# Second MLP's first layer: token tiles 0 and 1 as seven block products, accumulators kept in memory between stages

## The chip, the cores and the metric

One core of a Trainium2 chip. The metric is the time of one execution of the kernel on the device, in microseconds, lower is better. Before the change: median 592.0 us of 3 runs (591.9 to 592.14).

## The reference

`out = mlp2(mlp1(retention(q, k, v, lam)))` on 1536 tokens of width 512:

```
x = retention(q, k, v, lam)            # block-wise linear attention, 2 x 8 heads x 768 x 64
h = max(x @ w_in, 0);  x = (h * h) @ w_out          # first MLP:  512 -> 2048 -> 512
h = x @ w_in;          out = max(0.01 * h, h) @ w_out   # second MLP, leaky
```

The MLP weights come as 64-bit floats, everything else as 32-bit.

## The kernel before

**Precision.** A 32-bit operand is split into a high part (rounded to the matmul's format, `hi`) and the rest (`lo`); each product is three matmuls, hi x hi, hi x lo, lo x hi. ScalarE makes the high part, VectorE subtracts it from the source for the low part (`split`, L64).

**Tiling.** The tokens are three tiles of 512 (t = 0, 1, 2), the hidden width four stages of 512 columns (s = 0 to 3), for each of the two MLPs (l = 0, 1). `first(l, s, t)` (L379) makes a stage's hidden block: 4 column groups m x 4 inner blocks x 3 = 48 matmuls of 128x512 into four banks of the accumulator memory, each followed by the activation and the split into `ghi`, `glo`. `second` (L405) multiplies by the second weight, again 48 matmuls, and adds each of four banks to `acc`, which stays on chip over the stages.

**Order.** The list `line` (L446 to L451) sets the program: behind the first stage it alternates first of step i and second of step i-1, so that between a block's activation and its use a whole other tile of 48 matmuls lies. One step of weight work is put in at every fourth turn: `fetch` (L86) has SP load a quarter of a stage's weights (1024 KB of 64-bit words) and `converting` (L93) turns it into 32-bit hi and lo: on ScalarE the absolute value (L103) and the high part (L113), on VectorE seven operations on 128x1024, three of one input (L104, L105, L110) and four of two (L107, L111, L112, L114). The scheduler of the language orders each engine's instructions by its own estimate; TensorE and SP are in the written order only in the retention.

GpSimd works in the retention alone. Eight banks of accumulator memory are used in rotation (L58).

The functions that the diff touches follow with the line numbers of the profile.

## Time and profile before

| what | value |
|---|---|
| time, median of 3 runs | 592.0 us (591.9 to 592.14) |
| profiled execution: span from first to last instruction | 590.4 us |
| around the span (median less span) | 1.6 us |
| TensorE busy | 582.3 us, 99% |
| VectorE busy | 399.3 us, 68% |
| ScalarE busy | 253.3 us, 43% |
| GpSimd busy | 24.5 us, 4%, all before 60 us |
| granted TensorE clock, mean | 0.997 |

TensorE's busy time includes overlaps of pipelined matmuls; how fast it really goes is read from the distance between two matmuls in order of time. In the profile PE is TensorE, PEld its weight loads, DVE VectorE, ACT ScalarE, POOL GpSimd, SP the engine that issues the transfers.

### The profile page before, as it was taken

What the parts mean: (1) busy time and instruction counts of PE and PEld (TensorE: products, weight loads), DVE (VectorE), ACT (ScalarE), POOL (GpSimd) and SP (SyncE); (2) the same over time, 40 slices, a digit from 0 to 9 for tenths busy, and PEclk for the clock granted to TensorE, in tenths of its full rate; (3) what the DMA queues carried; (4) which work ended last, traced back from release to release, by engine and by line L of the source; (5) the groups of instructions that cost most, each with busy time, mean ns of one, the idle gap of its engine ahead of it and who ended that gap; (6) DMA issues with size and microseconds to landing.
All of it is one profiled execution on the core that took longest, in us unless ns stands there. A gap on an engine that the chain in (4) does not pass through costs nothing.

```text
span 590.4 us, 7683 instructions
## 1 busy us (share of the span) xinstructions
PE 582.3 (99%) x3147; PEld 485.9 (82%) x3147; DVE 399.3 (68%) x543; ACT 253.3 (43%) x379; POOL 24.5 (4%) x37
## 2 busy tenths in 40 slices
PE   7999999999999999999999999999999999999997
PEld 7888878888888888888888888888888888888886
DVE  3789499999979393856849793946779443344332
ACT  2344588458663372455373443536152223123120
POOL 2425000000000000000000000000000000000000
PEclk9999999999999999999999999999999999999999
DMA  8998133453343122040302212120400000000112
GB/s 175 240 211 205 67 101 113 153 180 115 124 142 89 54 72 71 2 143 0 143 1 72 71 68 75 46 98 1 142 1 0 1 0 2 0 1 0 72 53 90
DMA packets 57331, 47.17 MB, mean 80 GB/s; under 512 B 38216, under 2 KB 39504, under 8 KB 57296
## 3 DMA queue, kind: packets, MB, share of 16 engines
q1 hardware_dynamic: 56768, 46.41, 26.6%
q8 instruction: 25, 0.41, 0.3%
q10 hardware_dynamic: 528, 0.26, 0.2%
q14 instruction: 10, 0.08, 0.0%
HBM read 43.52 MB, written 3.15 MB: 79 GB/s over the span
## 4 chain that ended last, share of the span: by engine, by line
PE 94%; DVE 2%; DMA 1%; ACT 1%; issue 1%; POOL 0%; SPq 0%; POOLq 0%; ACTq 0%
PE ps L426 44%; PE ps L393 14%; PE ps L391 14%; PE ps L392 14%; PE ps L258 2%; PE ps L275 2%; PE ps L326 1%; DMA raw<-in_moe_w_in 1%; PE ps L324 1%; PE ps L299 1%; PE ps L184 1%; DVE glo L399 0%; ACT qT L262 0%; POOL kd L293 0%; SPq L62 0%
## 5 line engine op out<-in xcount | busy, mean ns | idle before, releaser
L391 PE MATMUL ps<-xhi,whi 128*128 128x512 f32 x384 | 149.6, 389 | 0.0
L393 PE MATMUL ps<-xhi,wlo 128*128 128x512 f32 x384 | 149.4, 389 | 0.2 <-DVE wlo L114 0.2
L392 PE MATMUL ps<-xlo,whi 128*128 128x512 f32 x384 | 149.4, 389 | 0.0
L431 DVE TENSOR_TENSOR acc<-ps,acc 128x512 f32<-128x512 f32 (+1 forms) x73 | 49.7, 681 | 61.9 <-PE ps L426 61.8
L393 PEld LDWEIGHTS ps<-xhi,wlo 128*128 128x128 f32 x384 | 72.1, 188 | 15.6 <-DVE wlo L114 0.6
L391 PEld LDWEIGHTS ps<-xhi,whi 128*128 128x128 f32 x384 | 72.1, 188 | 15.2 <-ACT whi L113 0.2
L392 PEld LDWEIGHTS ps<-xlo,whi 128*128 128x128 f32 x384 | 72.1, 188 | 15.0
L426 PE MATMUL ps<-wlo,ghi 128*128 128x512 f32 (+1 forms) x196 | 75.4, 385 | 0.0
L426 PE MATMUL ps<-whi,glo 128*128 128x512 f32 (+1 forms) x196 | 75.4, 385 | 0.0
L426 PE MATMUL ps<-whi,ghi 128*128 128x512 f32 (+1 forms) x196 | 75.4, 385 | 0.0
L401 ACT ACTIVATE r<-ps 128x512 f32<-128x512 f32 x48 | 28.7, 598 | 92.9 <-PE ps L393 92.8
L426 PE MATMUL ps<-ghi,whi 128*128 128x512 f32 x176 | 68.5, 389 | 0.0
L426 PE MATMUL ps<-glo,whi 128*128 128x512 f32 x176 | 68.5, 389 | 0.0
L426 PE MATMUL ps<-ghi,wlo 128*128 128x512 f32 x176 | 68.5, 389 | 0.0
L402 DVE TENSOR_TENSOR r<-ps,r 128x512 f32<-128x512 f32 x48 | 33.1, 689 | 33.0 <-ACT r L401 33.0
L396 ACT ACTIVATE r<-ps 128x512 f32<-128x512 f32 x48 | 28.5, 595 | 52.2 <-PE ps L393 51.7
L399 DVE TENSOR_TENSOR glo<-r,ghi 128x512 fp32r<-128x512 f32 x44 | 30.2, 688 | 30.4 <-ACT r L398 30.3
L114 DVE TENSOR_TENSOR wlo<-hb,whi 128x1024 fp32r<-128x1024 f32 x32 | 38.7, 1222 | 15.8 <-ACT whi L113 15.8
L113 ACT CAST whi<-hb 128x1024 fp32r<-128x1024 f32 x32 | 33.1, 1051 | 37.7 <-PE ps L426 27.4
L66 DVE TENSOR_TENSOR glo<-r,ghi 128x512 fp32r<-128x512 f32 x48 | 33.2, 691 | 22.2 <-ACT ghi L65 22.0
L65 ACT CAST ghi<-r 128x512 fp32r<-128x512 f32 x48 | 29.8, 621 | 37.5 <-DVE r L402 37.5
L103 ACT ACTIVATE hb<-raw 128x1024 f32<-128x1024 f32 x32 | 36.8, 1153 | 20.0 <-DMA raw<-in_moe_w_in 12.6
(78 smaller groups left out, 739.6 us busy)
## 6 DMA issues: line engine op xcount, KB each, us to landing
raw<-in_moe_w_in SPq DMA_DIRECT2D x16, 1024.0 KB, 5.5
raw<-in_moe_w_out SPq DMA_DIRECT2D x16, 1024.0 KB, 5.0
k<-in_k SPq DMA_DIRECT2D x12, 256.0 KB, 4.5
q<-in_q SPq DMA_DIRECT2D x12, 256.0 KB, 4.9
v<-in_v SPq DMA_DIRECT2D x12, 256.0 KB, 5.0
out<-acc SPq DMA_DIRECT2D x11, 256.0 KB, 2.0
DTr<-tab SPq DMA_DIRECT2D x1, 256.0 KB, 5.1
DTr<-tab ACTq DMA_DIRECT2D x1, 256.0 KB, 5.3
```

What stands on the lines that cost most here:

```text
L65: nc.scalar.copy(hi, src)
L66: nc.vector.tensor_tensor(out=lo, in0=src, in1=hi, op=ALU.subtract)
L103: nc.scalar.activation(hf, w_hi.bitcast(F32), AF.Abs)
L113: nc.scalar.copy(hi, hf)
L114: yield ve.tensor_tensor(out=lo, in0=hf, in1=hi, op=ALU.subtract)
L391: nc.tensor.matmul(ps, hi_w[:, kk, ms], xhi[t][:, kk], start=kk == 0, stop=False)
L392: nc.tensor.matmul(ps, hi_w[:, kk, ms], xlo[t][:, kk], start=False, stop=False)
L393: nc.tensor.matmul(ps, lo_w[:, kk, ms], xhi[t][:, kk], start=False, stop=kk == KD - 1)
L399: nc.vector.tensor_tensor(out=glo[:, m], in0=r, in1=ghi[:, m], op=ALU.subtract)
L402: nc.vector.tensor_tensor(out=r, in0=ps, in1=r, op=ALU.max)
L426: nc.tensor.matmul(ps, a, b, start=kk == 0 and n == 0, stop=kk == KF - 1 and n == 2)
L431: nc.vector.tensor_tensor(out=a, in0=ps, in1=a, op=ALU.add)
```

## The change

In the second MLP the first layer of tiles 0 and 1 is one job now, `first_pair(s)`. Weight and tokens are seen as 2 x 2 blocks: for each half h of a stage's columns (256) the weight blocks A11 to A22 (inner half j, 128 columns i), the tokens B11, B21 (tile 0, the two inner halves), B22 and B12 (tile 1). Four sums of weight blocks (S1 to S4) and four of token blocks (T1 to T4) are made, and seven products of six matmuls each take the place of eight. Their results are combined on VectorE in 32 bit: s1, s2 and r22 hold partial sums, and every block of tiles 0 and 1 is activated from there.

- `weight_sums` (in each stage, for each half) runs on GpSimd: four operations on 256 elements and two low parts on 512, with two high parts on ScalarE. `token_sums` (once, behind the first MLP) runs on GpSimd, four operations on 512 for each of two inner blocks, then splits on ScalarE and VectorE.
- The order of a stage is written out: in the first MLP `first` of tiles 0 and 1 by column halves, `second` of 0, `first` of 2, `second` of 1 and 2; in the second MLP `first_pair`, `second` of 0, `first` of 2, `second` of 1 and 2. At the end of the first MLP, `second` of tile 1 does column groups 0, 2, 1, then `first` of tile 2, then group 3, then `second` of tile 2. TensorE keeps the written order throughout.
- Weights are held by halves, w1 once, w2 three times; the conversion goes on one VectorE step at a time (`convert(1)` at each half group), except behind the last three pairs of products, and holds its last step until a buffer is free (`opened`).
- The second MLP's accumulators aren't kept on chip: after each stage each 128x512 block is written to memory (`spill`), and read back before the next stage's addition. A pool `fp` of nine 128x512 buffers serves all such plain values.

```diff
@@ converting
         yield ve.tensor_tensor(out=hf, in0=hf, in1=rf, op=ALU.add)
+        while key not in opened:
+            yield None
+        tags = (f"w1h{h}", f"w1l{h}") if n == 0 else ("w2h", "w2l")
+        bufs = 1 if n == 0 else 3
+        hi, lo = (wp.tile([P, 4 * CW], F32R, tag=tag, name=tag, bufs=bufs) for tag in tags)
         nc.scalar.copy(hi, hf)
...
         yield ve.tensor_tensor(out=lo, in0=hf, in1=hi, op=ALU.subtract)
+        if l == 1 and n == 0:
+            weight_sums(s, h, hf.rearrange("p (k f) -> p k f", k=k))
...
+    def weight_sums(s, h, w):
+        a = {(i, j): w[:, 2 * j:2 * j + 2, i * P:(i + 1) * P] for i in range(2) for j in range(2)}
+        both = late.tile([P, 2, 4, 2, P], F32R, tag=f"sw{h}", name=f"sw{h}")
...
+        po.tensor_tensor(out=f12[:, 0], in0=a[1, 0], in1=a[1, 1], op=ALU.add)
+        po.tensor_tensor(out=f12[:, 1], in0=f12[:, 0], in1=a[0, 0], op=ALU.subtract)
+        po.tensor_tensor(out=f34[:, 0], in0=a[0, 0], in1=a[1, 0], op=ALU.subtract)
+        po.tensor_tensor(out=f34[:, 1], in0=a[0, 1], in1=f12[:, 1], op=ALU.subtract)
+        for f, n in ((f12, 0), (f34, 2)):
+            nc.scalar.copy(both[:, 0, n:n + 2], f)
+            po.tensor_tensor(out=both[:, 1, n:n + 2], in0=f, in1=both[:, 0, n:n + 2], op=ALU.subtract)
+
+    def token_sums(j):
+        po = nc.gpsimd
+        a, b, c, d = x0f[j], x1f[j], x1f[j + 2], x0f[j + 2]
+        po.tensor_tensor(out=a, in0=b, in1=a, op=ALU.subtract)
+        po.tensor_tensor(out=b, in0=c, in1=b, op=ALU.subtract)
+        po.tensor_tensor(out=c, in0=c, in1=a, op=ALU.subtract)
+        po.tensor_tensor(out=d, in0=d, in1=c, op=ALU.subtract)
+        split(xhi[1][:, j], xlo[1][:, j], a)
+        for n, src in ((2, c), (3, b), (4, d)):
...
+            split(tt[n][:, 0, j], tt[n][:, 1, j], src)
+
+    def activate(l, src, r, ghi, glo):
...
+            if src is r:
+                nc.vector.scalar_tensor_tensor(out=r, in0=src, scalar=0.01, in1=src, op0=ALU.mult, op1=ALU.max)
+            else:
+                nc.scalar.mul(r, src, 0.01)
+                nc.vector.tensor_tensor(out=r, in0=src, in1=r, op=ALU.max)
+            nc.scalar.copy(ghi, r)
+        nc.vector.tensor_tensor(out=glo, in0=r, in1=ghi, op=ALU.subtract)
...
+    def first_pair(s):
...
+        def product(h, where, a, b, start=True):
+            if start:
+                ps[h, where] = bank()
+            (ah, al), (bh, bl) = w[h, a], x[b]
+            ops = []
+            for j in range(2):
+                ops += [(ah[:, j], bh[:, j]), (ah[:, j], bl[:, j]), (al[:, j], bh[:, j])]
+            three(ps[h, where], ops, start, True, not start)
+            return ps[h, where]
...
+        for h in both:
+            b = product(h, "A", "A11", "B11")
+            s1[h] = plain()
+            nc.scalar.copy(s1[h], b)
+            yield True
+        for h in both:
+            product(h, "B", "S2", "T2")
+            s2[h] = plain()
+            plus(h, s2[h], "B", s1[h])
+            yield True
+        for h in both:
+            product(h, "D", "A22", "T4")
+            yield True
+        for h in both:
+            product(h, "C", "S1", "T1")
+            yield True
+        for h in both:
+            product(h, "B", "S3", "T3", False)
+            plus(h, s1[h], "B", s1[h])
+            r22[h] = plain()
+            plus(h, r22[h], "C", s1[h])
+            plus(h, s1[h], "D", s1[h])
+            yield False
+        for h in both:
+            put(h, product(h, "A", "A12", "B21", False), plain(), 0, 0)
+            put(h, s1[h], s1[h], 1, 0)
+            yield False
+        for h in both:
+            product(h, "C", "S4", "B22", False)
+            plus(h, s2[h], "C", s2[h])
+            yield False
+        for h in both:
+            put(h, r22[h], r22[h], 1, 1)
+            put(h, s2[h], s2[h], 0, 1)
...
@@ second
+            if l == 1 and s and cs.start == 0:
+                spilled[m] = plain()
+                dma(spilled[m], spill[t][m])
...
+                if s == 0:
+                    spilled[m] = plain()
+                    nc.scalar.copy(spilled[m], ps)
+                else:
+                    a = spilled[m][:, cs]
+                    nc.vector.tensor_tensor(out=a, in0=ps, in1=a, op=ALU.add)
+                if last:
+                    r0 = t * TT + m * P
+                    dma(out[r0:r0 + P, cs], spilled[m][:, cs])
+                else:
+                    dma(spill[t][m], spilled[m])
...
+    def stage(l, s):
+        if (l, s) == (0, 0):
+            parts = [first(l, s, t, range(2)) for t in range(NTILE)]
+            parts += [first(l, s, t, range(2, 4)) for t in (0, 2, 1)]
+            return parts + [second(l, s, t) for t in (2, 0, 1)]
+        if l == 0:
+            parts = [first(l, s, t, ms) for ms in (range(2), range(2, 4)) for t in range(2)]
+        else:
+            parts = [first_pair(s)]
+        if (l, s) == (0, NS - 1):
+            return parts + [second(l, s, 0), second(l, s, 1, (0, 2, 1)), first(l, s, 2), second(l, s, 1, (3,)),
+                            second(l, s, 2)]
+        return parts + [second(l, s, 0), first(l, s, 2), second(l, s, 1), second(l, s, 2)]
```

**VectorE at the end of the products, second stage of the second MLP.** Before, the first layer of one tile: r is the activated block, glo its low part, hb, rb and wlo are weight conversion.

```order
L402 TENSOR_TENSOR r_3167<-ps_3154,r_3167 128x512
L66 TENSOR_TENSOR glo0_3104<-r_3167,ghi0_3103 128x512
L114 TENSOR_TENSOR wlo00_3322<-hb_3356,whi00_3321 128x4x256
L402 TENSOR_TENSOR r_3185<-ps_3172,r_3185 128x512
L114 TENSOR_TENSOR wlo00_3322<-hb_3435,whi00_3321 128x4x256
L66 TENSOR_TENSOR glo0_3104<-r_3185,ghi0_3103 128x512
```

Now, around the ninth to twelfth product: ps are the banks of the products, f_3445 and f_3460 are s1 of half 0 and 1, f_3530 and f_3540 r22, f_3549 and f_3563 the block that needs no combination, g0l the low parts of tile 0.

```order
L513 TENSOR_TENSOR f_3445<-ps_3463,f_3445 128x512
L116 SCALAR_TENSOR_TENSOR rb_3733<-raw_3517,rb_3733 128x1024
L513 TENSOR_TENSOR f_3530<-ps_3499,f_3445 128x512
L513 TENSOR_TENSOR f_3460<-ps_3473,f_3460 128x512
L513 TENSOR_TENSOR f_3445<-ps_3483,f_3445 128x512
L513 TENSOR_TENSOR f_3540<-ps_3510,f_3460 128x512
L448 TENSOR_TENSOR f_3549<-ps_3438,f_3549 128x512
L513 TENSOR_TENSOR f_3460<-ps_3491,f_3460 128x512
L445 SCALAR_TENSOR_TENSOR f_3445<-f_3445 128x512
L450 TENSOR_TENSOR g0l_3435<-f_3549,g0h_3434 128x512
L448 TENSOR_TENSOR f_3563<-ps_3453,f_3563 128x512
L450 TENSOR_TENSOR g0l_3435<-f_3445,g0h_3434 128x512
```

The same queue goes on with the leaky operation on half 1 and the sums s2:

```order
L445 SCALAR_TENSOR_TENSOR f_3460<-f_3460 128x512
L450 TENSOR_TENSOR g0l_3435<-f_3563,g0h_3434 128x512
L513 TENSOR_TENSOR f_3470<-ps_3499,f_3470 128x512
L450 TENSOR_TENSOR g0l_3435<-f_3460,g0h_3434 128x512
L513 TENSOR_TENSOR f_3480<-ps_3510,f_3480 128x512
L445 SCALAR_TENSOR_TENSOR f_3530<-f_3530 128x512
```

Before, a block's maximum and split came one after the other with conversions between; now six sums (L513) stand ahead of the first low part of tile 0 (L450), and a sum for tile 1 (f_3470) ahead of its last.

**TensorE behind the first layer, the same stage.** Before: tile 0's first layer ends (x are tokens, whi00 and wlo00 first weights), and what follows is the second layer of the tile before it.

```order
L392 MATMUL ps_3303<-xlo0_2558,whi01_2863 128x512
L393 MATMUL ps_3303<-xhi0_2557,wlo01_2864 128x512
L426 MATMUL ps_3328<-whi10_2399,ghi0_3103 128x512
L426 MATMUL ps_3328<-wlo10_2400,ghi0_3103 128x512
L426 MATMUL ps_3328<-whi10_2399,glo0_3104 128x512
```

Now: the last product (sw1 are the weight sums of half 1, xhi1 holds T1 and B22) and behind it tile 0's own second layer, whose third matmul reads a low part.

```order
L454 MATMUL ps_3510<-xhi1_2655,sw1_3312 128x512 x2
L454 MATMUL ps_3510<-xlo1_2656,sw1_3312 128x512
L454 MATMUL ps_3510<-xhi1_2655,sw1_3312 128x512
L454 MATMUL ps_3599<-w2h_3016,g0h_3434 128x512
L454 MATMUL ps_3599<-w2l_3017,g0h_3434 128x512
L454 MATMUL ps_3599<-w2h_3016,g0l_3435 128x512
```

A tile's second layer moved from a whole tile behind its first to right behind it.

**GpSimd.** Before, its last work is the retention's.

```order
L293 TENSOR_TENSOR kd_933<-k_679,kdec_170 128x512
L306 TENSOR_TENSOR tmp_894<-st1_174,LR_169 64x256 x2
L306 TENSOR_TENSOR tmp_944<-st0_172,LR_169 64x256 x2
L483 UNCONDITIONAL_BRANCH
L483 ISA
```

Now the layer change follows: f are token sums (L428 to L431) of inner block 1, f_2769 to f_2872 weight sums from the converted weights hb, sw0 and sw1 the low parts.

```order
L428 TENSOR_TENSOR f_2617<-f_2717,f_2617 128x512
L416 TENSOR_TENSOR f_2769<-hb_2504 128x256
L418 TENSOR_TENSOR f_2770<-hb_2504 128x256
L417 TENSOR_TENSOR f_2769<-f_2769,hb_2504 128x256
L419 TENSOR_TENSOR f_2770<-hb_2504,f_2769 128x256
L422 TENSOR_TENSOR sw0_2768<-f_2769,sw0_2768 128x512
L422 TENSOR_TENSOR sw0_2768<-f_2770,sw0_2768 128x512
L416 TENSOR_TENSOR f_2871<-hb_2781 128x256
L418 TENSOR_TENSOR f_2872<-hb_2781 128x256
L417 TENSOR_TENSOR f_2871<-f_2871,hb_2781 128x256
L419 TENSOR_TENSOR f_2872<-hb_2781,f_2871 128x256
L429 TENSOR_TENSOR f_2717<-f_2831,f_2717 128x512
```

The weight sums of both halves stand ahead of the second token sum of inner block 1 (L429), which waits for the last column group of tile 1.

## Rows read from the trace of the kernel before

**Rows 1.** The page: header, busy time of the engines (share) xinstructions, chain by engine.
```profile
span 590.4 us, 7683 instructions
...
PE 582.3 (99%) x3147; PEld 485.9 (82%) x3147; DVE 399.3 (68%) x543; ACT 253.3 (43%) x379; POOL 24.5 (4%) x37
...
PE 94%; DVE 2%; DMA 1%; ACT 1%; issue 1%; POOL 0%; SPq 0%; POOLq 0%; ACTq 0%
```

**Rows 2.** Busy time by engine from the first MLP matmul to the last addition.
```profile
core 0: us, PE busy (x) PEld busy (x) DVE busy (x) ACT busy (x) POOL busy (x), PEclk, DMA share, GB/s
63.50:587.00 523.50, 523.15 (x2318) 432.96 (x2316) 351.81 (x447) 228.83 (x338) 0.00 (x0) 1.00 0.19 64
```

**Rows 3.** The chain in order of time (start us, us, what): one tile.
```profile
151.48 10.88 PE ps L426 x48
```

**Rows 4.** TensorE by time (start, length, engine line op) near 81 us.
```profile
80.76 0.40 PE L392 MATMUL ps<-xlo,whi 128*128 128x512 f32 x1
81.33 0.50 PE L393 MATMUL ps<-xhi,wlo 128*128 128x512 f32 x1 [0.18 <-DVE wlo L114]
81.67 0.40 PE L391 MATMUL ps<-xhi,whi 128*128 128x512 f32 x1
```

**Rows 5.** VectorE in order of time, the change from retention to the MLPs.
```profile
68.60 0.69 DVE L399 TENSOR_TENSOR glo<-r,ghi 128x512 fp32r<-128x512 f32 x1 [2.79 <-ACT r L398]
71.32 0.69 DVE L399 TENSOR_TENSOR glo<-r,ghi 128x512 fp32r<-128x512 f32 x1 [2.03 <-ACT r L398]
71.93 0.69 DVE L104 TENSOR_SCALAR hb<-hb 128x1024 f32<-128x1024 f32 x1
```

**Rows 6.** VectorE in order of time, a full stretch of the second MLP.
```profile
342.63 0.68 DVE L66 TENSOR_TENSOR glo<-r,ghi 128x512 fp32r<-128x512 f32 x1
343.23 0.68 DVE L402 TENSOR_TENSOR r<-ps,r 128x512 f32<-128x512 f32 x1
343.83 1.21 DVE L107 SCALAR_TENSOR_TENSOR hb<-raw,hb 128x1024 uint32<-128x1024 uint32 x1
344.96 0.68 DVE L66 TENSOR_TENSOR glo<-r,ghi 128x512 fp32r<-128x512 f32 x1
...
351.53 1.22 DVE L107 SCALAR_TENSOR_TENSOR hb<-raw,hb 128x1024 uint32<-128x1024 uint32 x1
352.78 0.70 DVE L110 TENSOR_SCALAR rb<-hb 128x1024 uint32<-128x1024 uint32 x1
```

**Rows 7.** VectorE, then ScalarE, in turn at two blocks (second MLP).
```profile
361.65 0.69 DVE L402 TENSOR_TENSOR r<-ps,r 128x512 f32<-128x512 f32 x1 [5.65 <-ACT r L401]
363.03 0.69 DVE L66 TENSOR_TENSOR glo<-r,ghi 128x512 fp32r<-128x512 f32 x1 [0.69 <-ACT ghi L65]
...
362.38 0.62 ACT L65 CAST ghi<-r 128x512 fp32r<-128x512 f32 x1 [0.76 <-DVE r L402]
```

**Rows 8.** ScalarE on one block of the first MLP; VectorE follows at 68.60.
```profile
66.64 0.60 ACT L396 ACTIVATE r<-ps 128x512 f32<-128x512 f32 x1 [1.55 <-PE ps L393]
...
67.94 0.63 ACT L398 ACTIVATE r<-r 128x512 f32<-128x512 f32 x1
```

**Rows 9.** GpSimd, then VectorE, beside each other in the retention.
```profile
31.34 1.04 POOL L293 TENSOR_TENSOR kd<-k,kdec 128x512 f32<-128x512 f32 x1 [3.42 <-DMA k<-in_k]
33.33 0.62 POOL L306 TENSOR_TENSOR tmp<-st,LR 64x256 f32<-64x256 f32 x1 [0.96 <-DVE st L311]
...
47.37 2.00 POOL L293 TENSOR_TENSOR kd<-k,kdec 128x512 f32<-128x512 f32 x1 [1.02 <-issue]
...
31.35 1.58 DVE L104 TENSOR_SCALAR hb<-hb 128x1024 f32<-128x1024 f32 x1 [1.58 <-ACT hb L103]
...
47.26 1.21 DVE L111 SCALAR_TENSOR_TENSOR rb<-raw,rb 128x1024 f32<-128x1024 uint32 x1
```

**Rows 10.** DMA issues of the page: engine op xcount, KB each, us to landing.
```profile
raw<-in_moe_w_in SPq DMA_DIRECT2D x16, 1024.0 KB, 5.5
...
out<-acc SPq DMA_DIRECT2D x11, 256.0 KB, 2.0
```

More of the change, by code (lines that the diff above doesn't have):

```diff
@@ L86, in fetch @@
+    order = [(0, 0, 0, 0), (0, 0, 0, 1), (0, 0, 1, 0), (0, 0, 1, 1)]
+    stages = [(l, s) for l in range(2) for s in range(NS)]
+    for before, stage in zip(stages, stages[1:]):
+        if before != stages[0]:
+            order.append((*before, 1, 1))
+        order += [(*stage, 1, 0), (*stage, 0, 0), (*stage, 0, 1)]
+    order.append((*stages[-1], 1, 1))
+    todo = list(order)
+    fetched, at_work = [], []
+    wts, sums, opened = {}, {}, set()
     def fetch():
         if todo:
-            src, hi, lo = todo.pop(0)
@@ L134, in convert @@
                     tc.keep_in_program_order(step)
-    wts, todo, fetched = {}, [], []
-    place = [early, None]
-    load_w(0, 0)
+    begun_mlp = []
+    opened.update(order[:5])
     xhi = [None] * NTILE
@@ L439, in tile_retention_then_two_mlps @@
-    steps = [(l, s, t) for l in range(2) for s in range(NS) for t in range(NTILE)]
+                convert(1, pin=True)
     with ExitStack() as ctx_att:
@@ L443, in tile_retention_then_two_mlps @@
             retention(ctx_att, att)
-    place[1] = ctx.enter_context(tc.tile_pool(name="late", bufs=1, reuse_waits="tile"))
-    begun = [first(*steps[t]) for t in range(NTILE)]
-    line = [islice(work, KF // 2 + 1) for work in begun] + [begun[0], begun[2], begun[1]]
-    line += [second(*steps[2]), second(*steps[0]), second(*steps[1]), first(*steps[3])]
-    for i in range(4, len(steps)):
-        line += [first(*steps[i]), second(*steps[i - 1])]
-    line.append(second(*steps[-1]))
-    turn = 0
@@ new lines, in tile_retention_then_two_mlps, with new_g @@
+    spilled = {}
+    g, acc, x0f, x1f, tt = {}, [None] * NTILE, {}, {}, {}
+    def new_g(t, first_stage=False):
+        if first_stage and t == 2:
+            tags = ("sw0", "sw1")
+        else:
+            tags = (f"g{t % 2}h", f"g{t % 2}l")
+        g[t] = [late.tile([P, KF, TT], F32R, tag=tag, name=tag) for tag in tags]
+    def weight_sums(s, h, w):
+        a = {(i, j): w[:, 2 * j:2 * j + 2, i * P:(i + 1) * P] for i in range(2) for j in range(2)}
+        both = late.tile([P, 2, 4, 2, P], F32R, tag=f"sw{h}", name=f"sw{h}")
+        sums[s, h] = both
+        f12, f34 = (plain().rearrange("p (n k f) -> p n k f", n=2, k=2) for _ in range(2))
+        po = nc.gpsimd
[6 more added lines that the diff above has]
+            po.tensor_tensor(out=both[:, 1, n:n + 2], in0=f, in1=both[:, 0, n:n + 2], op=ALU.subtract)
@@ new lines, in three, with first @@
+    def three(ps, ops, start, stop, again=False):
+        for n, (a, b) in enumerate(ops):
+            nc.tensor.matmul(ps, a, b, start=start and n == 0, stop=stop and n == len(ops) - 1, skip_group_check=again)
+    def first(l, s, t, ms=range(KF)):
+        for m in ms:
+            if m == 0:
+                new_g(t, (l, s) == (0, 0))
+            ghi, glo = g[t]
+            hi, lo = wts[l, s, 0, m // 2]
+            cs = slice(m % 2 * P, (m % 2 + 1) * P)
+            ps = bank()
+            ops = []
+            for kk in range(KD):
+                ops += [(hi[:, kk, cs], xhi[t][:, kk]), (hi[:, kk, cs], xlo[t][:, kk]), (lo[:, kk, cs], xhi[t][:, kk])]
+            three(ps, ops[:6], True, False)
+            yield
+            three(ps, ops[6:], False, True)
+            activate(l, ps, plain(), ghi[:, m], glo[:, m])
+            if t == 2 and m % 2:
+                opened.add((*stages[stages.index((l, s)) + 1], 0, m // 2) if (l, s) != stages[-1] else None)
+            yield
@@ L465 @@
+    begun_mlp.append(True)
+    opened.update(order[:7])
+    with tc.manual_schedule(engines={mybir.EngineType.PE}):
+        for l, s in stages:
+            for part in stage(l, s):
+                for room in part:
+                    if room is not False:
+                        convert(1)
 _INS = ["q", "k", "v", "lam", "moe_w_in", "moe_w_out", "moe2_w_in", "moe2_w_out"]
```

212 lines of the change are left out of this document (113 added, 99 removed).

## Prediction

> **What bounds the kernel now.** I read the page's header and chain first: TensorE is busy 582.3 of 590.4 us and the chain of waits lies 94% on it [rows 1]. Then the windows: from 63.5 us, where the MLPs begin, to 587 us TensorE is busy in 523.15 of 523.50 us at clock 1.00, while VectorE works 351.81 us, 67%, and GpSimd nothing at all [rows 2]. Then the chain in order of time: 48 matmuls of 512 columns, one token tile through one layer of a stage, take 10.88 us [rows 3], so one matmul costs 10.88 / 48 = 0.2267 us. The one place inside the MLPs where TensorE waits is at 80.8 to 81.3 us [rows 4]: after the row at 80.76 the next comes 0.57 us later and the one after that 0.34 later, where 0.23 each is the pace, so about 0.45 us is lost to the second half of the first weights. The reader is to see that a matmul taken away is worth its 0.2267 us in full, and that any wait put into TensorE's stream costs its whole length.
>
> The profiled execution lasted 590.4 us by its span; the median of the runs is 592.0, so 1.6 us lie around the span. I sum against the span and add these 1.6.
>
> **What goes.** Per stage of the second MLP, tiles 0 and 1 had 2 x 4 x 12 = 96 matmuls in the first layer; seven products for two halves of the columns, six matmuls each, are 84. Four stages: 48 matmuls, 48 x 0.2267 = 10.88 us. The order of the two programs agrees: 2791 matmuls before, 2743 now. Accumulating a second product into a bank that was read in between (S3, A12, S4) appears in no row; I take the same 0.2267, since operands and shape are those of the rows. Bounds: no gain is possible below that pace, and a loss of one matmul's latency, 0.40 instead of 0.23 [rows 4], on 24 such products would be 4 us.
>
> In the first stage the second weight half is now converted while the retention ends; before, its conversion began at 71.93, and VectorE idled 2.79 and 2.03 us just before [rows 5]. So the 0.45 us of rows 4 goes too. What is late next there, the second layer's second weight half, has some 13 us of VectorE operations behind that half, and is wanted 18 us after it (seven and a half groups of 2.72 us): no new wait.
>
> **What comes on VectorE, and where it lies.** A stage of the second MLP had 16 VectorE operations for tiles 0 and 1 (maximum and split per block); now 26 (ten additions more). Two operations in a row that don't depend on each other follow at 0.60 us for 512 elements and 1.13 us for 1024, though they are recorded as 0.68 and 1.21; one that needs the one before waits for its end, and one input on 1024 is recorded like two on 512 [rows 6]. Per stage that is 4 conversions x (4 x 1.13 + 3 x 0.60) + 46 x 0.60 = 25.3 + 27.6 = 53 us in 276 x 0.2267 = 62.6 us of matmuls. It fits, so what counts is where TensorE waits for the last of it: **the end of the seven products**. Before, a tile's second layer came one whole tile (10.88 us) after its first. Now tile 0's second layer follows its products directly, and ten operations of combination stand ahead of its inputs on VectorE.
>
> I walk the second stage along VectorE's new order (the first piece of order in the section on the change). Zero is when the ninth product, S3 x T3 of half 0, can be read; a product is 6 x 0.2267 = 1.36 us. VectorE comes free at about 0.4 from the conversions. Then: s1 0.4, a conversion 1.0 to 2.1, r22 2.1, the other s1 2.7, + D 3.3, r22 3.9, maximum 4.5, + D 5.1, leaky 5.7, first low part 6.3, maximum 6.9, second low part 7.5, leaky 8.1, third low part 8.7, s2 9.3, fourth low part 9.9; each result is there 0.69 later, and ScalarE's copy between (0.62, hand-over 0.03 [rows 7]) fits in. So the low parts are ready at 7.0, 8.2, 9.4 and 10.6. TensorE issues the last product's last matmul at 6.6 and wants them with its third, sixth, ninth and twelfth matmul after it: 7.1, 7.8, 8.5, 9.1. It waits 0.5 three times, and loses 0.1 more after the last wait, as the matmul of 0.50 after a wait shows [rows 4]: 1.6 us. The same walk for the other stages: 2.75 in the first (both r22 and a weight half ahead of the low parts, an s2 pair ahead of the fourth), 1.2 in the third (no backlog at zero), 0.45 in the last (no conversions left). Sum 6.0 us. Bounds: zero if VectorE and ScalarE are early enough everywhere; 11.2 if each operation costs its recorded 0.69 and 1.22 us instead of the pace. I take the pace, since rows 6 are such a queue of mixed operations. The leaky operation (one operand twice, 512 elements) is in no row; half of a 1024-element one of its kind (1.13) and its fixed part give 0.60, bounds 0.53 and 0.69.
>
> **The layer change.** Tile 2's second layer now comes only one group of 2.72 us after its first, and the activation chain of the first MLP is three ScalarE operations and one on VectorE, 2.65 us undisturbed [rows 8]. But ScalarE and VectorE also carry the sums' splits and the weights there (the piece of order on GpSimd). Tile 2's last low part is wanted 2.72 + 11 matmuls after the first layer's end, 5.2 us. From the first block on ScalarE has the four blocks' twelve operations, some 7 us by rows 8, and between them four on 512 and three on 1024 for the weights, some 4 us more if these cost what VectorE's do; it starts 1.5 us late, behind GpSimd's first sums, and VectorE follows it: I get the low part 2.0 us late, and 0.3 us more at T4's split. I take 2.3 in all; below, 0.3 if GpSimd and VectorE don't disturb each other; above, 5.
>
> That disturbance is in the rows [rows 9]: a GpSimd operation of 1.04 us took 2.00 where it began inside a VectorE operation with both inputs in SBUF (47.26 to 48.47), and a VectorE operation of 0.69 took 1.58 where GpSimd began 0.01 us earlier. The Trainium skill (SBUF — State Buffer, Who interferes with whom) says that the two engines' shared ports are an exclusive lock, taken for a whole instruction by a two-port mode of VectorE or by one with two SBUF inputs against a GpSimd read; the trace agrees (2.00 and 1.58 us above), and the low parts, weight splits and leaky operations are all of that kind. By that rule the new sums on GpSimd are VectorE's time as well, and the sum would be the slow rival's; without it, it stays as it is.
>
> **What is hidden.** GpSimd's 12 weight sums a stage are 8 x 0.62 + 4 x 1.04 = 9.1 us [rows 9] and lie beside tile 2's first layer and tile 1's second, 17 us before they are wanted; cover gone, up to 9.1 us a stage. The spilled accumulators add 36 writes and 36 reads of 256 KB on SP's queue; a write of that size lands in 2.0 us, a weight quarter of 1024 KB in 5.5 [rows 10]. A read is issued when its buffer of the nine comes free, at the latest about 13 after the zero above, while its addition is due near 20; behind it on SP stand the next reads and weight quarters, which are wanted a stage later. If a read is late, VectorE waits, not TensorE, which has eight banks: bounds 0 and some 3 us in each of three stages; I take 0. The first MLP's new order keeps two groups (5.4 us) between a block and its use: 0.
>
> **Sum.** 590.4 - 10.9 - 0.45 + 6.0 + 2.3 = 587.4 us of span, so 589.0 us.
>
> **Rivals.** (1) *VectorE keeps up.* Every stage's tail costs what the last one's does (4 x 0.45 = 1.8) and the layer change 0.3: 592.0 - 11.3 + 2.1 = 582.8. For it: 33% of VectorE is idle [rows 2]. Against: that idle time lies before the products end, not behind. (2) *The waits eat the gain.* VectorE's steps cost 0.69 and 1.22: 592.0 - 11.3 + 11.2 + 0.5 = 592.4, no change that can be measured. For it: half of the tail's steps are dependent; against: the queue of rows 6. (3) *Slower: GpSimd's sums take VectorE's ports.* Each of the three stages that prepare weights loses up to 9.1 us of VectorE time, 53 + 9 = 62 of 62.6 us; with its waits for ScalarE (0.69 us a block [rows 7]) it is then late, conversions slip into the next tail, and from 2.4 us of lateness at the zero on (the ten additions have no slack left) the tail grows one for one. At 3 us a stage and 5 at the layer change: 592.0 - 11.3 + 6.0 + 9 + 5 = 600.7; with half of both 593.7. For it: rows 9. Against: in the walk VectorE has idle time late in each stage, where the sums lie. That the change doesn't do what it says I leave out: the matmuls are counted.
>
> **Chances.** Forecast (586 to 591) 0.52, rival 1 0.13, rival 2 0.13, rival 3 0.22. A difference of 0.2%, 1.2 us, is about what a measurement of this kernel tells from none: faster is below 590.8, slower above 593.2. Faster: rival 1 and nine tenths of the forecast, 0.60; no change: rival 2 and the rest, 0.18; slower 0.22. The forecast's own range is 586 to 591; for 8 in 10 I reach from rival 1 to the milder half of rival 3: 583 to 596.
>
> **What would show it.** In the changed profile: 2268 matmuls of the MLPs at the same 10.88 us per 48; TensorE idle only at four places between the products and tile 0's second layer, by 2.8, 1.6, 1.2 and 0.5 us, each ended by VectorE's low part; about 2.3 us at tile 2's second layer at the layer change; no wait at the second weight half of the first stage; no TensorE wait for a spilled read. I am wrong if TensorE waits inside the products for GpSimd's sums, if VectorE's fast operations grow well beyond 0.69 beside GpSimd in every stage, or if the tails cost nothing.

## The result, and the profile after

The changed kernel takes 597.3 us (median of 4 runs, 596.7 to 598.5), the kernel before, on the same chip, 592.1: 1.0088 times, with an interval of 1.0076 to 1.0100. It is 0.9% slower, where 589.0 us and faster had been predicted. The profiled execution has a span of 594.9 us; the sum of the prediction came to 587.4. I compare spans in what follows, and look for 7.5 us.

The page of the changed kernel, the lines that answer to [rows 1] and, below them, the transfers of [rows 10]:

```profile
span 594.9 us, 7911 instructions
...
PE 580.2 (98%) x3099; PEld 479.3 (81%) x3099; DVE 444.8 (75%) x589; ACT 254.6 (43%) x385; POOL 102.6 (17%) x93
...
PE 82%; DVE 11%; ACT 2%; issue 2%; POOL 1%; DMA 1%; POOLq 0%; DVEq 0%; ACTq 0%; SPq 0%
...
spill<-f SPq DMA_DIRECT2D x36, 256.0 KB, 2.2
f<-spill SPq DMA_DIRECT2D x36, 256.0 KB, 2.9
```

The 48 matmuls are gone (3147 before, 3099 now), but the chain of waits, which lay 94% on TensorE, lies 82% there and 11% on VectorE. It leaves TensorE at the ends of the seven products, and for longest at the layer change, the passage from the first MLP to the second. The windows show it (us, busy time and count by engine, granted clock, DMA share, GB/s); they are to be read against [rows 2]:

```profile
63.50:591.00 527.50, 519.50 (x2264) 425.04 (x2263) 396.72 (x490) 230.25 (x344) 76.99 (x56) 0.99 0.30 100
...
312.00:316.00 4.00, 3.28 (x15) 2.39 (x13) 3.19 (x4) 3.97 (x6) 2.54 (x2) 1.00 0.00 0
316.00:320.00 4.00, 1.73 (x5) 1.04 (x6) 4.00 (x6) 0.80 (x3) 2.81 (x3) 0.73 0.00 0
320.00:324.00 4.00, 4.00 (x11) 3.13 (x10) 3.89 (x4) 3.21 (x6) 4.00 (x3) 0.50 0.00 0
324.00:328.00 4.00, 4.00 (x17) 3.25 (x17) 4.00 (x5) 1.67 (x4) 3.23 (x4) 0.92 0.00 0
328.00:332.00 4.00, 4.00 (x19) 3.30 (x19) 4.00 (x5) 0.53 (x2) 1.73 (x2) 1.00 0.03 9
...
336.00:340.00 4.00, 1.89 (x5) 1.06 (x5) 3.17 (x6) 2.63 (x4) 0.00 (x0) 0.79 0.01 2
...
312.00:344.00 32.00, 26.89 (x98) 20.49 (x97) 30.25 (x35) 15.60 (x24) 14.31 (x10) 0.84 0.11 34
```

And the last of these windows in the kernel before:

```profile
312.00:344.00 32.00, 32.00 (x143) 26.47 (x142) 27.67 (x39) 14.15 (x22) 0.00 (x0) 1.00 0.20 66
```

The largest loss is the layer change, 312 to 344 us; the rest, at the ends of the products, follows below. VectorE is busy nearly without a break there, GpSimd works beside it, and TensorE stands still and then runs at a granted clock of 0.50, the lower of its two levels (1.2 GHz). From 320 to 324 us it counts as busy for all 4 us and still has only 11 matmuls, where the window at full clock from 328 to 332 has 19: here the busy share hides the loss, and the clock's column shows it. TensorE by time, at tile 2's second layer and at the product A22 x T4:

```profile
314.89 0.39 PE L454 MATMUL ps<-g0h,w2h 128*128 128x512 f32 x1
317.09 0.51 PE L454 MATMUL ps<-g0l,w2h 128*128 128x512 f32 x1 [1.81 <-DVE g0l L450]
...
317.67 0.50 PE L454 MATMUL ps<-g0h,w2h 128*128 128x512 f32 x1
319.35 0.80 PE L454 MATMUL ps<-g0l,w2h 128*128 128x512 f32 x1 [1.18 <-DVE g0l L450]
319.94 0.63 PE L454 MATMUL ps<-g0h,w2l 128*128 128x512 f32 x1
320.37 0.63 PE L454 MATMUL ps<-g0h,w2h 128*128 128x512 f32 x1
...
338.11 0.67 PE L454 MATMUL ps<-t,w1h 128*128 128x512 f32 x1 [1.96 <-ACT t L68]
338.94 0.80 PE L454 MATMUL ps<-t,w1h 128*128 128x512 f32 x1 [0.16 <-DVE t L69]
```

After the two waits the next matmuls follow at 0.43 us instead of 0.23. In the written order, tile 2's second layer (48 matmuls) runs from 313.53 to 330.55, 17.0 us for 10.9 of pace; the first six products (36) from 330.55 to 342.83, 12.3 for 8.2. The layer change costs 6.1 + 4.1 = 10.3 us (before rounding), some 6 of it standing still and some 4 at half clock. Now what VectorE does before and between the two waits:

```profile
310.96 1.36 DVE L450 TENSOR_TENSOR g0l<-f,g0h 128x512 fp32r<-128x512 f32 x1 [0.77 <-ACT f L442]
313.06 0.97 DVE L109 TENSOR_SCALAR hb<-hb 128x1024 f32<-128x1024 f32 x1 [0.74 <-ACT hb L108]
314.06 1.11 DVE L110 TENSOR_SCALAR hb<-hb 128x1024 uint32<-128x1024 uint32 x1
315.20 1.23 DVE L112 SCALAR_TENSOR_TENSOR hb<-raw,hb 128x1024 uint32<-128x1024 uint32 x1
316.35 0.69 DVE L450 TENSOR_TENSOR g0l<-f,g0h 128x512 fp32r<-128x512 f32 x1
316.95 1.22 DVE L126 TENSOR_TENSOR w1l<-hb,w1h 128x1024 fp32r<-128x1024 f32 x1
318.08 1.21 DVE L450 TENSOR_TENSOR g0l<-f,g0h 128x512 fp32r<-128x512 f32 x1
...
320.61 0.69 DVE L591 TENSOR_TENSOR acc<-ps,acc 128x512 f32<-128x512 f32 x1
321.22 1.66 DVE L69 TENSOR_TENSOR t<-f,t 128x512 fp32r<-128x512 f32 x1
322.80 1.78 DVE L69 TENSOR_TENSOR xlo<-f,xhi 128x512 fp32r<-128x512 f32 x1
```

And GpSimd in the same microseconds:

```profile
310.47 3.00 POOL L422 TENSOR_TENSOR sw<-f,sw 128x512 fp32r<-128x512 f32 x2 [1.36 <-ACT sw L421]
...
321.05 1.27 POOL L429 TENSOR_TENSOR f<-f 128x512 f32<-128x512 f32 x1
322.29 1.74 POOL L422 TENSOR_TENSOR sw<-f,sw 128x512 fp32r<-128x512 f32 x1
```

The low parts at L450 and the splits at L69 took 0.68 or 0.69 us in the kernel before [rows 6]; beside a sum on GpSimd they take 1.2 to 1.8. The third low part, wanted at 315.1, starts at 316.35, behind three steps of a weight's conversion, two of them stretched as well (0.97 and 1.11 for 0.69, with one input). I call "stretch" what VectorE's operations last beyond 0.69 us (512 elements, or 1024 with one input) or 1.22 (1024 with two), added up over those that are more than 0.1 us longer. From 296 to 356 us there is none in the kernel before, and 8.5 us in this one: 2.6 before 312 us, 5.9 behind. (Two expectations below say 9.2 and 6.6: they count the operation at 310.96 twice.)

The addition at 320.61, with one input in accumulator memory, is not stretched. The Trainium skill (SBUF — State Buffer, Who interferes with whom) draws that line: a VectorE instruction with two inputs in SBUF contends with a GpSimd instruction that reads SBUF, one with at most one such input, outside the two-port modes, does not. The trace agrees: 0.69 against 1.66 and 1.78. Whether the conversions at 313.06 and 314.06, stretched with one input, ran in such a mode no run shows.

The last link before T4's split was not a VectorE operation but a weight's transfer, as the chain shows (start us, us, what):

```profile
330.88 5.47 DMA raw<-in_moe_w_in
...
336.43 1.14 ACT hb L108
```

T4's sums were done at 328.04, and the memory that it takes was free at 336.16, but on ScalarE its split stands behind this step, which waited 0.93 us for the transfer; the split began at 337.45. The transfer itself was issued when VectorE had read the buffer's old content at L116, which took 2.30 us there for 1.22.

The rest of the prediction stands. TensorE in the second stage's tail (one of four places):

```profile
419.17 0.39 PE L454 MATMUL ps<-w2l,g0h 128*128 128x512 f32 x1
...
420.66 0.50 PE L454 MATMUL ps<-w2h,g0l 128*128 128x512 f32 x1 [0.24 <-DVE g0l L450]
...
421.87 0.50 PE L454 MATMUL ps<-w2h,g0l 128*128 128x512 f32 x1 [0.24 <-DVE g0l L450]
...
423.07 0.50 PE L454 MATMUL ps<-w2h,g0l 128*128 128x512 f32 x1 [0.23 <-DVE g0l L450]
423.40 0.40 PE L454 MATMUL ps<-w2h,g0h 128*128 128x512 f32 x1
```

From 419.17 to 423.40 are eleven steps, 4.2 us where the pace makes 2.5: 1.7 us lost. By the same reading the four tails cost 2.6, 1.7, 1.4 and 0.5 us, 6.2 together. At 81 us, where [rows 4] had a wait, the matmuls now follow without one:

```profile
80.97 0.39 PE L454 MATMUL ps<-xhi,w1h 128*128 128x512 f32 x1
81.19 0.39 PE L454 MATMUL ps<-xlo,w1h 128*128 128x512 f32 x1
81.42 0.39 PE L454 MATMUL ps<-xhi,w1l 128*128 128x512 f32 x1
```

### The profile page after: what moved, and what is told of

It reads as the page before. It is cut to its first block, busy times and chain, and to the rows that moved or that the text cites. A ratio compares the mean times of both kernels' runs of the same rounds, so it can differ in the third digit from the quotient of the medians.

```text
span 594.9 us, 7911 instructions
## 1 busy us (share of the span) xinstructions
PE 580.2 (98%) x3099; PEld 479.3 (81%) x3099; DVE 444.8 (75%) x589; ACT 254.6 (43%) x385; POOL 102.6 (17%) x93
## 4 chain that ended last, share of the span: by engine, by line
PE 82%; DVE 11%; ACT 2%; issue 2%; POOL 1%; DMA 1%; POOLq 0%; DVEq 0%; ACTq 0%; SPq 0%
PE ps L454 73%; DVE f L513 2%; PE ps L273 2%; PE ps L290 2%; DVE g0l L450 2%; PE ps L341 2%; PE ps L339 2%; PE ps L314 1%; DMA raw<-in_moe_w_in 1%; DVE xlo L69 1%; DVE rb L116 1%; DVE f L448 1%; DVE f L445 1%; DVE hb L112 1%; PE ps L199 1%
## 5 line engine op out<-in xcount | busy, mean ns | idle before, releaser
L454 PE MATMUL ps<-xhi,w1h 128*128 128x512 f32 x288 | 112.3, 390 | 0.0
L454 PE MATMUL ps<-xhi,w1l 128*128 128x512 f32 x288 | 112.2, 390 | 0.0
L454 PE MATMUL ps<-xlo,w1h 128*128 128x512 f32 x288 | 112.2, 389 | 0.0
L450 DVE TENSOR_TENSOR g0l<-f,g0h 128x512 fp32r<-128x512 f32 x60 | 48.3, 808 | 20.5 <-ACT f L442 16.4
L454 PEld LDWEIGHTS ps<-xhi,w1h 128*128 128x128 f32 x288 | 54.1, 188 | 11.4 <-issue 0.2
L454 PEld LDWEIGHTS ps<-xhi,w1l 128*128 128x128 f32 x288 | 54.1, 188 | 11.2
L454 PEld LDWEIGHTS ps<-xlo,w1h 128*128 128x128 f32 x288 | 54.1, 188 | 11.1
L454 PE MATMUL ps<-w2h,g0l 128*128 128x512 f32 (+1 forms) x132 | 51.8, 392 | 2.3 <-DVE g0l L450 2.2
L454 PE MATMUL ps<-w2h,g0h 128*128 128x512 f32 (+1 forms) x132 | 50.9, 385 | 0.6 <-ACT g0h L449 0.6
L454 PE MATMUL ps<-w2l,g0h 128*128 128x512 f32 (+1 forms) x132 | 50.6, 384 | 0.0
L428 POOL TENSOR_TENSOR f<-f 128x512 f32<-128x512 f32 x2 | 3.0, 1522 | 236.1 <-DVE f L584 236.1
L116 DVE SCALAR_TENSOR_TENSOR rb<-raw,rb 128x1024 f32<-128x1024 uint32 x32 | 41.6, 1299 | 0.4
```

The source lines that it names most:

```text
L116: yield ve.scalar_tensor_tensor(out=rf, in0=w_lo, scalar=2.0 ** -52, in1=rf, op0=ALU.mult, op1=ALU.mult)
L450: nc.vector.tensor_tensor(out=glo, in0=r, in1=ghi, op=ALU.subtract)
L454: nc.tensor.matmul(ps, a, b, start=start and n == 0, stop=stop and n == len(ops) - 1, skip_group_check=again)
```

## The experiments

All start from the changed kernel, and times are medians. Ratios are to the kernel before, measured on the same chip; the changed kernel's is 1.0088. Each expectation names a theory and a rival with the time that each would give, and a side, below, is one of the two. The scheduler orders every engine but TensorE anew in each kernel, so that an edit also moves operations it doesn't name: T4's split, for one, stands behind a weight's conversion step on ScalarE in some of these kernels and ahead of it in others.

**First group: what makes the layer change slow?** My theory was too little cover: one group of 2.72 us between tile 2's layers, and then the clock.

*More cover* (`e1_cover`).

```diff
-second(l, s, 1, (0, 2, 1)), first(l, s, 2), second(l, s, 1, (3,)),
+second(l, s, 1, (0, 2)), first(l, s, 2), second(l, s, 1, (1, 3)),
```

> Only the order of the matmuls at the layer change differs: two groups of tile 1 instead of one (5.44 us instead of 2.72) stand between tile 2's first and second layer. Theory (too little cover, the wait then doubled by the clock): tile 2's second layer, 48 matmuls, which took 17.0 us in the changed kernel for 10.9 of pace, takes 11 to 12; the clock there stays at 1.00; the wait for T4 (4.1 us over the pace) keeps 1 to 4 us. Time 591.5 to 593.5 us. Rival, GpSimd's sums hold VectorE's ports so that the low parts are late whatever stands before them: less than 2 us come back, 595.5 or more.

598.5 us, 1.0091 (1.0070 to 1.0112): no gain. The first wait did go, and another took its place, as the waits of TensorE in this run say (us in total, times, longest):

```profile
PE ps L454 <- ACT t L68: 6.9, 2, 4.7
...
PE ps L454 <- DVE g0l L450: 1.9, 8, 0.2
```

2.0 us of waiting for T4 have become 6.9 for the token sums' splits. The theory of cover fell.

*The weight sums of that stage on VectorE* (`e3_vector`).

```diff
-        po = nc.gpsimd
+        po = nc.vector if s == 0 else nc.gpsimd
```

> The twelve weight sums of the first stage of the second MLP run on VectorE instead of GpSimd; all others stay. Rival (the port lock makes VectorE late at the layer change): low parts and splits there fall back to 0.69 us, the 10.3 us over the pace shrink by 4 or more, 593 us or less. Theory (VectorE's and ScalarE's queues are full there, the lock is a small part): VectorE gets some 6 us of sums into the same stretch, the low parts become later, 596 to 601 us.

595.6 us, 1.0051 (1.0034 to 1.0067): neither side. It is 1.6 us faster than the changed kernel by the medians; the profiled execution, the slowest of the four, has the same span, 594.9. The stretch fell from 8.5 to 2.5 us, and the sums added about 5.1 us of VectorE's own (8 at 0.34 and 4 at 0.60, from start to start). So on GpSimd these sums cost VectorE about what they would cost it as its own work.

*Matmuls in the waits* (`e4_filler`; `filler(n, ...)` does n matmuls into a bank that nobody reads).

```diff
+            if (l, s, t, m) == (0, NS - 1, 2, 0):
+                filler(8, ghi[:, 0])
+                three(ps, ops[6:9], False, False)
+                filler(5, ghi[:, 0])
+                three(ps, ops[9:], False, True)
...
+            if (s, h, b) == (0, 0, "T4"):
+                for i in range(8):
+                    nc.tensor.matmul(ps[h, where], ah[:, 0], x["B11"][0][:, 0], start=i == 0, stop=i == 7)
```

> Matmuls whose result nobody reads fill TensorE's waits at the layer change: 8 before the matmul that waits for tile 2's third low part, 5 before the fourth, 8 before A22 x T4 (21 x 0.2267 = 4.8 us at full clock, about as long as the waits). Theory (some 3.6 us of the 10.3 are the halved clock after the waits): the granted clock stays near 1.00 from 316 to 344 us and 2 to 4 us come back, 593.5 to 595.5 us. Rival (the clock follows something else, or the slower matmuls were hidden by the waits): no gain, 597 to 599 us.

600.0 us, 1.0119 (1.0104 to 1.0134): slower than the changed kernel, which neither side had. Windows of this run, columns as above:

```profile
316.00:320.00 4.00, 3.85 (x16) 2.57 (x15) 4.00 (x5) 1.09 (x2) 2.53 (x2) 1.00 0.00 0
320.00:324.00 4.00, 4.00 (x19) 3.29 (x19) 3.96 (x4) 1.94 (x4) 3.92 (x4) 1.00 0.09 24
...
336.00:340.00 4.00, 0.00 (x0) 0.00 (x0) 4.00 (x7) 2.39 (x4) 0.00 (x0) 0.84 0.01 2
```

The clock stayed at 1.00 over the first place, as wanted, and nothing came of it: at T4 TensorE then waited 5.4 us and did no matmul from 336 to 340, while VectorE was busy. So the half clock of the changed kernel was not a loss by itself: with it gone there, the next wait grew by as much and more.

*S1 x T1 ahead of A22 x T4* (`e5_swap`; the two loops of `first_pair` change places).

> In all four stages the products S1 x T1 stand ahead of A22 x T4 (2.72 us more for T4's split). Theory: the second loss of the layer change (4.1 us: 2.4 to 3 waiting for T4, the rest at half clock) shrinks to 0 to 1.5 us; the first (6.1 us) stays; the tails stay within 1 us in sum. 593.5 to 595.5 us. Rival (T4's split waits behind the copy of the first product and a weight's load, not for time): the wait only moves by 2.7 us and the slack it leaves is less than 1 us, 596.5 us or more.

596.6 us, 1.0063 (1.0048 to 1.0078), span 595.0. The rival's number, by another way: the wait for T4 is gone, and one of 2.9 us for VectorE's additions (L513) stands three products later. Four edits had now moved the wait and hardly shortened the program, or lengthened it: what is late is not one input but VectorE.

**Second group: VectorE's time, or GpSimd's?**

*No sums on GpSimd* (`e6_nosums`).

```diff
+        if s == 0:
+            for part in range(2):
+                nc.scalar.copy(both[:, part].rearrange("p n k f -> p (n k f)"), w.rearrange("p k f -> p (k f)"))
+            return
...
-        po.tensor_tensor(out=a, in0=b, in1=a, op=ALU.subtract)
-        po.tensor_tensor(out=b, in0=c, in1=b, op=ALU.subtract)
-        po.tensor_tensor(out=c, in0=c, in1=a, op=ALU.subtract)
-        po.tensor_tensor(out=d, in0=d, in1=c, op=ALU.subtract)
```

> Left out: the twelve weight sums of the second MLP's first stage (two copies on ScalarE per half take their place) and the eight token sums; every split, conversion and product stays. GpSimd then does nothing at the layer change. Theory now (VectorE is the bound there from 306 to 353 us, and 9.2 us of its time in the changed kernel, 2.6 before 312 us and 6.6 after, are operations stretched beside GpSimd): the 10.3 us over the pace shrink to 1 to 3.5, 588 to 590.5 us. Rival (VectorE's own added splits and the order are enough; the stretch fell into idle time): 7 us or more stay, 594 us or more.

This kernel leaves the sums out, and TensorE does the same products on operands that are not summed. 585.0 us, 0.9883 (0.9868 to 0.9898), below the theory's range: 11.7 us of span came back, nearly the whole layer change and 1.8 of the first tail's 2.6. The stretch is 0.4 us, and from 312 on VectorE's operations follow without idle time; still TensorE waits hardly at all:

```profile
312.00:344.00 32.00, 31.80 (x141) 26.02 (x140) 31.93 (x46) 16.06 (x24) 0.00 (x0) 1.00 0.21 66
```

VectorE's own work there just fits; with GpSimd beside it, it doesn't.

*Less conversion* (`e7_light`; six steps of one weight quarter are left out).

```diff
+        if key == (1, 0, 1, 1):
+            for _ in range(6):
+                yield True
+        else:
```

> Left out: the six VectorE steps of one weight quarter (first stage of the second MLP, second layer, second half), which run between 313 and 332 us; 3 x 1.13 + 3 x 0.60 = 5.2 us of VectorE at its pace. GpSimd's sums stay. Theory (VectorE's time is the bound, whatever takes it): 4 to 6 us come back, 591 to 593.5 us. Rival (only the chain through GpSimd and ScalarE to T4 and the low parts counts, VectorE's load does not): less than 1.5 us come back, 595.5 us or more.

595.7 us, 1.0060 (1.0045 to 1.0075): the rival's side. The first waits fell to 1.05 and 0.40 us and the clock stayed at 1.00 behind them, but the wait for T4 grew to 5.2. VectorE idled 6.1 us between 312 and 356, so its load alone is not the bound either: the way to T4 leads through GpSimd's sums, tile 2's last splits (T4 takes the memory of tile 2's accumulator) and VectorE in turn, and VectorE's steps are stretched there (4.4 us behind 312).

*Tile 1 finished first* (`e8_order`; and tile 2's second layer takes low halves last).

```diff
-second(l, s, 1, (0, 2, 1)), first(l, s, 2), second(l, s, 1, (3,)),
+second(l, s, 1, (0, 2, 1, 3)), first(l, s, 2),
```

> In the last stage of the first MLP tile 1's second layer is finished before tile 2's first layer begins, so that the token sums start some 11 us earlier, into stretches where VectorE idles 5.6 of 16 us; tile 2's second layer follows its first without cover, but works on the high halves of all four blocks first (32 matmuls, 7.3 us) and on the low ones last. Theory (VectorE's time is the bound and must be moved to where it idles): 4 to 7 us come back, 590 to 593 us. Rival (whatever the order, the sums stretch VectorE by as much, and its idle time cannot be used because the weights' conversions come later): 596 us or more.

600.8 us, 1.0147 (1.0131 to 1.0164): the rival's side, and slower still. The stretch is 8.4 us as before; without cover TensorE now also waits 3.5 us for high parts of ScalarE.

*Low halves last in the tails* (`e9_lowlast`; in `second`, for l = 1 and t = 0).

```diff
+            for kk in range(KF):
+                for m, cs in groups:
...
+                        ops = [(ghi[:, kk, ms_], hi[:, cs]), (ghi[:, kk, ms_], lo[:, cs])]
+                        lows.setdefault(m, []).append((glo[:, kk, ms_], hi[:, cs]))
+                    three(pss[m], ops, kk == 0, False)
```

> The second MLP's second layer of tile 0 takes the high halves of all four blocks first (32 matmuls, 7.3 us) and the low halves last, in all four stages; the layer change stays. Theory (the tails are 5.9 us of TensorE waiting for low parts that come at most 2.8 us late): the tails fall to 0 to 1.5 us in sum, 591.5 to 593 us. Rival (four banks held at once, or four spilled reads and additions close together, bring a new wait in each stage): 595 us or more.

592.2 us, 0.9990 (0.9975 to 1.0006; ten runs, 589.8 to 593.8), as expected: 5.1 us faster than the changed kernel by the medians, for tails of 6.2. At the four places 0.3 us is left in the first, and nothing in the others.

**Third group: a version without the loss.**

*Weight sums one stage earlier* (`f1_early`). They need the converted half, not its split, so they can come before the step that waits for a buffer; the second half's conversion runs beside the waiting first one.

```diff
+        if (l, s, n) == (1, 0, 0):
+            weight_sums(s, h, hf.rearrange("p (k f) -> p k f", k=4))
         while key not in opened:
             yield None
...
+            if step is None and len(at_work) == 1 and fetched and fetched[0][0] == (1, 0, 0, 1):
+                at_work.append(converting())
+            if step is None and len(at_work) == 2:
+                step = next(at_work[1], None)
```

> The twelve weight sums of the second MLP's first stage stay on GpSimd but are made as soon as their weight half is in floating point, one stage earlier (around 285 to 296 us, where VectorE idles), by letting the second half's conversion run beside the waiting first one. The token sums stay. Theory (GpSimd's sums stretch VectorE's operations where VectorE has no idle time, and that is the loss of the layer change): the stretch after 312 us falls from 6.6 to 2 to 3 us, the layer change from 10.3 to 3 to 6 us over the pace, 590.5 to 594 us. Rival (what counts is the chain through GpSimd's token sums to T4, whatever else GpSimd does): 595 us or more.

592.4 us, 1.0005 (0.9993 to 1.0017), span 590.7: as the theory had it. From 296 us on the stretch is 2.8 us instead of 8.5. TensorE still waits 1.2 us for a low part and 3.0 for T4.

*Tile 2's last additions in other buffers* (`f3_t4f`).

```diff
-                    nc.vector.tensor_tensor(out=a, in0=ps, in1=a, op=ALU.add)
+                    f = plain() if last else a
+                    nc.vector.tensor_tensor(out=f, in0=ps, in1=a, op=ALU.add)
```

> Tile 2's last additions go to buffers of the nine instead of in place into its accumulator, whose memory T4 takes over: T4's splits need no longer wait for the last split of tile 2, only for its last addition. Theory (T4's wait is the lateness of VectorE, the buffer a small part): 0.5 to 2 us back, 595 to 597 us. Rival (the buffer is the cause of the second wait, since T4's first half was ready at 304 us and is split at 337): the wait for T4 goes, 4 us back, 593.5 us or less.

596.3 us, 1.0066 (1.0046 to 1.0085): the theory's side, 1.0 us faster than the changed kernel by the medians, with intervals that overlap. TensorE still waits 3.1 us for T4, so its buffer is at most a small part.

*Three edits together* (`f5_all`: `f1_early`, `f3_t4f`, `e9_lowlast`), *and the token sums on VectorE* (`f6_allvec`: `po = nc.vector` in `token_sums`).

> Three edits together: the first stage's weight sums early, tile 2's last additions in other buffers, and in the second MLP's second layer of tile 0 the low halves last. Theory: the layer change costs 2 to 5 us over the pace instead of 10.3, the tails 0 to 1 instead of 5.9; 583 to 588 us. Rival (the gains do not add up: what leaves one wait turns up in the next, as with more cover and with the filler): 589 us or more.

> As the three edits together, and the eight token sums on VectorE as well, so that GpSimd does nothing near the layer change. Theory (a sum on GpSimd costs VectorE about as much by stretch as it would take there, seen when the weight sums were moved): within 1.5 us of the kernel with the token sums on GpSimd. Rival (the lock costs more than the work): 2 us or more faster.

585.6 us, 0.9880 (0.9861 to 0.9899), and 581.2 us, 0.9808 (0.9793 to 0.9824). The first as expected. For the second the theory was wrong: moving eight sums to VectorE brought 4.4 us more, beyond the stretch that was left (2.8). They are also done sooner there, 0.68 to 0.69 us each against 1.28 and more on GpSimd, which may be the rest; no run separates it. Page and windows of the second:

```profile
span 579.3 us, 7912 instructions
...
PE 572.1 (99%) x3099; PEld 477.5 (82%) x3099; DVE 445.5 (77%) x597; ACT 255.7 (44%) x385; POOL 88.9 (15%) x85
```

```profile
312.00:344.00 32.00, 32.00 (x140) 25.85 (x139) 31.75 (x46) 15.33 (x24) 0.00 (x0) 1.00 0.20 66
360.00:570.00 210.00, 210.00 (x928) 173.96 (x927) 166.93 (x210) 71.33 (x107) 47.16 (x35) 1.00 0.42 139
```

VectorE is 99% busy through the layer change and TensorE doesn't wait there; one wait of 0.4 us for a high part is left behind the first products. 590.4 - 10.9 - 0.45 = 579.05: the span of 579.3 is the change's whole gain with next to nothing given back.

**Fourth group: which sums, and what of the other stages?**

*Token sums alone on VectorE* (`g1_tokens`), *and these with the early weight sums and nothing else* (`g2_earlytok`).

> Only the eight token sums go from GpSimd to VectorE; the weight sums stay on GpSimd at the layer change, the tails stay. Theory A (two losses of their own: the weight sums' stretch of VectorE, and the token sums' slow way to T4): some 4 us back, as the token sums brought in the kernel with all three edits; 592 to 594.5 us. Theory B (the weight sums alone fill VectorE there, and whatever is freed is taken up by the next wait): 595.5 us or more.

> Token sums on VectorE and the first stage's weight sums early; tails, tile 2's accumulator and order of products as in the changed kernel: nothing but GpSimd's part in the layer change is undone, and no sum is left out. Theory (that part is the whole of the layer change's loss and of 2 us in the first tail): 585 to 587 us, as in the kernel without the sums. Rival (the sums' own time on VectorE, 4.8 us for tokens, is not covered): 588.5 us or more.

594.3 us, 1.0038 (1.0023 to 1.0053), and 587.7 us, 0.9929 (0.9912 to 0.9945). The first is on theory A's side. The second lies between its two ranges; in the trace no wait is left at the layer change but one of 0.2 us, and the first tail costs 3.0, which in the kernel without sums had been 0.8. Its span is 9.6 us below the changed kernel's; by itself each move brought 4.2 (weights) and 2.5 (tokens): one alone leaves a wait that the other would have ended.

*All sums on VectorE* (`g3_allvector`).

> The fastest kernel so far (three edits, token sums on VectorE), with the weight sums of all four stages on VectorE too: GpSimd does nothing in the MLPs. Prediction's slow rival (in each stage the sums take VectorE's time through the ports): 1 to 9 us faster than 581.2. Theory (in the stages VectorE has idle time where the sums lie, and the stretch falls there): 580.5 to 583 us, the sums' some 5 us a stage on VectorE being hidden as well.

582.1 us, 0.9830 (0.9815 to 0.9845): the theory's side. In this kernel GpSimd does nothing from 360 to 570 us and there is no stretch there; in the changed kernel it was 13.7 us:

```profile
360.00:570.00 210.00, 210.00 (x928) 173.82 (x927) 168.21 (x247) 71.32 (x107) 0.00 (x0) 1.00 0.41 139
```

And in the changed kernel:

```profile
360.00:570.00 210.00, 208.53 (x911) 170.20 (x910) 171.21 (x216) 74.36 (x114) 50.57 (x36) 1.00 0.41 137
```

VectorE has 39 and 42 us without work in that stretch; the stretch falls there and costs TensorE nothing in the kernel with the low halves last. In the changed kernel no run takes it away in these stages alone; the three tails there are close to what the walk gave without any stretch.

## Why the prediction was wrong

**Right.** 48 matmuls at the pace (10.9). The wait at 81 us gone (0.45). The tails, by size and place: 2.6, 1.7, 1.4 and 0.5 us against 2.75, 1.6, 1.2 and 0.45; taking them away gave 5.1 us back. No wait of TensorE names a spilled read, which lands in 2.9 us. The products that go on in a bank already read showed no cost of their own: in the fastest kernel they run at the pace. The program's counts of 2791 and 2743 matmuls stand in no profile, but the profile's, 3147 and 3099, differ by the same 48. Two slips changed nothing: 18 us are six and a half groups of 2.72, not seven and a half, and 6.6 in the walk is the place of the first matmul behind the products, not of their last.

**Wrong: one term of the sum, the layer change**, put at 2.3 us with bounds of 0.3 and 5. It cost 10.3. With 6.2 for the tails and 10.3 for this, 590.4 - 10.9 - 0.45 + 6.2 + 10.3 = 595.5, against a span of 594.9. Three steps made it too small:

- The walk gave VectorE's operations there their lengths of a stretch in which GpSimd is idle, and counted GpSimd's sums only as a start 1.5 us late. Beside GpSimd's sums VectorE's operations were 8.5 us longer. [Rows 9] had shown the pair (2.00 for 1.04 us, 1.58 for 0.69); I used them in the slow rival only.
- T4's split was put at 0.3 us. It stands at the end of a chain through GpSimd, VectorE and, last, a weight's transfer and its first step on ScalarE, and cost 4.1 with the half clock behind it.
- The half clock after a wait was in no term. It is some 4 of the 10.3 us. It wasn't a further loss, though: kept away by the filler, its time came back as waiting.

**The slow rival named the mechanism.** It had 5 us at the layer change and 3 us in each of three stages. At the layer change it was right and too small; in the stages the stretch is there (13.7 us in the three) and no cost of it was found: VectorE has idle time at those places, as the prediction had held against this rival. So one of the prediction's own signs of being wrong, fast operations far beyond 0.69 us in every stage, came true without being what made it wrong. That the sums on GpSimd cause the loss at the layer change is shown by leaving them out (11.7 us of span back) and by moving them (9.6), in both cases with the stretch gone or nearly gone. The weight's transfer ahead of T4's split is not what makes T4 late: with more cover, with the weight sums on VectorE, with the filler and with less conversion the split follows VectorE's last split of tile 2 instead, and TensorE waits 4.7 to 5.4 us for it. How the loss divides between stretch on VectorE and GpSimd's own slowness on the way to T4 is not settled to the microsecond: the two moves brought more together than apart.

My first theory in the experiments, too little cover, was wrong as well: more cover, another order and a filler each took one wait away, and the next input of the same late engine took its place.

## What to carry to other kernels

Before side work goes to an idle engine, ask what it shares with the engine that follows it in the chain: here a sum on GpSimd cost VectorE as much as doing the sum itself, so it is free only where VectorE idles. When an edit removes a wait and the time stays, stop moving waits and add up the work of the engine that ends them, at the lengths that operations have in that very stretch. Sums that need only an early input belong at that input, and of a split operand the half that is ready first should be used first for all blocks.

## What was not expected of the hardware

After waits of 1.81 and 1.18 us with three matmuls between, TensorE's granted clock fell to its lower level for 6.8 us, and again, for 3.4 us, after 1.96 us at T4; after single waits of 1.2 and 1.5 us in the kernel with three edits it stayed at 1.00. GpSimd is held up as well: its sum of 256 elements (L418) took 1.64 us at 317.11, where VectorE's weight split of 316.95 was under way, and 0.73 at 305.96, where it had begun just before VectorE's next operation.
